# A fused retention and feed-forward kernel: constants and stores on GpSimd's DMA queue, one activation table, another order of weight pieces, chunk transposes and PSUM banks

## The chip, the cores and the metric

The kernel runs on one core of one Trainium2 chip. The metric is the device time of one execution in microseconds (us). The profile's span is about 1.8 us shorter than the time of the same execution, so I compare spans with spans and times with times.

Names: PE is TensorE's matmuls, PEld its weight loads, DVE is VectorE, ACT is ScalarE, POOL is GpSimd, SP is the engine that issues most DMAs. "ACTq" or "SPq" is such an engine's instruction queue. "[1.87 <-DVE W L372]" behind a line of the timeline means that the engine stood idle for 1.87 us until VectorE's instruction at line 372, which writes W, was done.

## The reference

Attention with a decaying state over four batches, eight heads and 768 steps, followed by a feed-forward layer with a sigmoid gate:

```python
gamma = 1.0 - 2.0 ** (-5.0 - np.arange(H))          # one decay per head
for t in range(S):
    state = gamma * state + outer(k[t], v[t])        # per batch and head, 64 x 64
    y[t]  = q[t] @ state / sqrt(D)
x = y.transpose(0, 2, 1, 3).reshape(B * S, H * D)    # 3072 x 512
h = x @ w_in                                         # 512 x 2048
out = (h / (1 + exp(-1.702 * h))) @ w_out            # 2048 x 512
```

(I have shortened it; q, k and v are float32 and the weights come as 64-bit floats, which the kernel narrows itself.)

## The kernel before

Time is cut into 24 chunks of 128 steps and these into six blocks of four chunks. For each chunk, TensorE transposes q and k (`turn`, line 225), makes scores (`pa`, line 257), VectorE multiplies them with a decay mask (line 263), TensorE makes the output and the state's update (lines 284 and 292, `finish`), and VectorE scales the output into `X` (line 296). The feed-forward layer of block 0 runs in units of 16 matmuls (`up0`, line 329); block 1 follows in `up1` (line 342). The later blocks and the product with `w_out` for all blocks (`pd`, line 432) take up most of the span.

The front, roughly the first 43 us: there the weights are fetched in pieces and each piece is narrowed from 64 to 32 bits by one ScalarE and six VectorE instructions:

```python
def narrow():                                       # lines 188 to 198, shortened
    act.activation(m, hi, AF.Abs, scale=2.0 ** 16)                      # L188
    dve.tensor_scalar(m, m, MOST, LEAST, op0=min, op1=max)              # L189
    dve.tensor_scalar(mu, mu, 3, None, op0=shift_left)                  # L191
    dve.scalar_tensor_tensor(hi, hi, SIGN, mu, op0=and, op1=or)         # L192
    dve.tensor_scalar(mu, hi, 0xFF800000, None, op0=and)                # L193
    dve.scalar_tensor_tensor(lo, lo, 2.0 ** -52, m, op0=mult, op1=mult) # L194
    dve.tensor_add(w, hi, lo)                                           # L198
    fetch()                                         # the next piece's DMA
```

The first two calls take half pieces (128 x 512), the later ones 128 x 1024. The loop that interleaves them with the first four chunks, before the change:

```python
load(0)
act.dma_start(cold, ...)                            # column decays
act.dma_start(rowd[...], ...)                       # row decays, two DMAs
act.dma_start(whole[...], ...)                      # four small DMAs
fetch(); load(1); fetch()
make_identity(nc, ident)
# ... mask from cold, 7 idle transposes
turn(0, ...)
for j in range(CB):                                 # CB = 4
    attend(j)
    narrow()
    turn(j + 1)
    # ...
    attend(None, j)                                 # finish(j); the last one with chunk 4's scores
    if j == 0: narrow()
    else:      up0(0, j - 1, "x")
for n, unit in enumerate(...):
    up0(*unit, "xy"[n % 2])                         # PSUM tag of each half unit
```

A PSUM tag ("x" or "y") has two buffers. The transposes of q and k use tag "y".

## Time and profile before

| | before |
|---|---|
| time, median | 711.3 us |
| span of the profiled run | 711.2 us |
| TensorE busy | 685.9 us, 96% |
| VectorE busy from 24 to 40 us | 14.66 of 16 us |

The profiled execution took 712.99 us, 1.7 more than the median. TensorE is the bound nearly everywhere, so the time is TensorE's busy time plus its holes. The prediction below shows the lines on which that rests. Two lines of VectorE's timeline before belong beside them: the X of chunk 0 and the mask product of chunk 3, which releases chunk 4's scores on TensorE (the third line).

```profile
17.29 0.69 DVE L296 TENSOR_TENSOR X<-py,rowd 128x512 f32<-128x512 f32 x1 [0.92 <-PE py L292]
...
43.19 1.27 DVE L263 TENSOR_TENSOR G<-pa,mask 128x512 f32<-128x512 f32 x2
...
44.61 1.10 PE L257 MATMUL pa<-G 64*64 64x128 f32 x32 [1.68 <-DVE G L263]
```

Chunk 4's scores on TensorE start at 44.61. I use that place as the end of the front, since TensorE is nearly always busy after it.

### The profile page before, as it was taken

The page shows a single profiled execution, that of the slowest core. Times are in us where ns is not written, and L with a number is a line of the kernel's source. Part 1 is how long each engine was busy: PE and PEld are TensorE (multiplying, and loading weights), DVE is VectorE, ACT ScalarE, POOL GpSimd, SP SyncE. Part 2 cuts the span into 40 slices and gives each one's busy share as a digit, 9 for nine tenths or more (in the row PEclk, how much of TensorE's full clock was granted, in tenths as well). Part 3 has the DMA queues.
Part 4 walks back from the last instruction along what each step waited for, and adds up shares of the span by engine and source line. Part 5 has one row for each costly group of instructions (what it writes and reads, how often), then busy time and mean ns, then how long its engine had stood idle before and what let it go on. Part 6 is the DMA issues. An engine that isn't in the chain of part 4 may idle for free.

```text
span 711.2 us, 11031 instructions
## 1 busy us (share of the span) xinstructions
PE 685.9 (96%) x4493; PEld 572.1 (80%) x4493; DVE 361.3 (51%) x520; ACT 126.5 (18%) x197; POOL 111.1 (16%) x99
## 2 busy tenths in 40 slices
PE   6689999999989999999999999999999999999997
PEld 5577776446878888888888888888888888888886
DVE  2997879995621652344463345264345272344241
ACT  2312222321000000332000233000233000233000
POOL 2221000000266221100132200032200042000030
PEclk9999999999999999999999999999999999999999
DMA  9996442521211224300333300323310220100001
GB/s 200 246 228 173 134 133 75 185 35 32 43 35 45 53 47 88 68 1 6 72 59 84 77 3 2 62 46 72 76 30 1 32 58 2 44 1 1 15 1 44
DMA packets 143602, 46.36 MB, mean 65 GB/s; under 512 B 130752, under 2 KB 137408, under 8 KB 143552
## 3 DMA queue, kind: packets, MB, share of 16 engines
q1 hardware_dynamic: 134704, 38.84, 23.9%
q10 hardware_dynamic: 8848, 6.83, 3.1%
q8 instruction: 35, 0.57, 0.3%
q14 instruction: 15, 0.12, 0.1%
HBM read 39.33 MB, written 6.29 MB: 64 GB/s over the span
## 4 chain that ended last, share of the span: by engine, by line
PE 81%; DVE 9%; SPq 5%; DMA 2%; issue 2%; ACT 1%; ACTq 0%; DVEq 0%
PE pd L432 34%; PE px L381 15%; PE py L381 11%; PE ph L342 8%; PE ph L329 5%; SPq L132 5%; PE py L284 3%; PE pa L257 3%; PE py L292 1%; PE py L282 1%; DVE G L371 1%; DVE W L198 1%; DVE G L263 1%; DMA W<-in_moe_w_in_dram 1%; DMA kn_in<-in_k_dram 1%
## 5 line engine op out<-in xcount | busy, mean ns | idle before, releaser
L432 PE MATMUL pd<-W,G 128*128 128x256 f32 x1120 | 247.4, 381 | 0.4 <-DVE G L372 0.3
L432 PEld LDWEIGHTS pd<-W,G 128*128 128x128 f32 x1120 | 211.3, 190 | 30.6 <-DVE G L372 1.2
L381 PE MATMUL px<-X,W 128*128 128x256 f32 x512 | 119.1, 379 | 1.2 <-ACT p L388 1.2
L381 PEld LDWEIGHTS px<-X,W 128*128 128x128 f32 x512 | 97.1, 190 | 14.9 <-POOL X L356 1.6
L381 PE MATMUL py<-X,W 128*128 128x256 f32 x384 | 90.7, 379 | 0.0
L381 PEld LDWEIGHTS py<-X,W 128*128 128x128 f32 x384 | 73.0, 190 | 9.9
L329 PE MATMUL ph<-X,W 128*128 128x256 f32 x256 | 57.9, 383 | 4.8 <-ACT G L226 4.1
L263 DVE TENSOR_TENSOR at<-pa,mask 128x512 f32<-128x512 f32 x32 | 21.7, 686 | 79.6 <-PE py L284 70.8
L329 PEld LDWEIGHTS ph<-X,W 128*128 128x128 f32 x256 | 47.8, 190 | 12.3 <-ACT G L226 4.8
L342 PE MATMUL ph<-W,W 128*128 128x512 f32 x128 | 55.1, 592 | 0.0
L244 POOL TENSOR_TENSOR kd<-kn_in,cold 128x512 f32<-128x512 f32 x13 | 13.6, 1044 | 237.5 <-PE py L292 182.4
L342 PEld LDWEIGHTS ph<-W,W 128*128 128x128 f32 x128 | 24.3, 190 | 30.2 <-issue 29.2
L373 POOL TENSOR_TENSOR G<-G 128x512 f32<-128x512 f32 x20 | 29.5, 1484 | 118.2 <-DVE G L372 115.4
L310 DVE TENSOR_TENSOR G<-G,sg 128x512 f32<-128x512 f32 x48 | 33.1, 689 | 14.0 <-ACT sg L308 14.0
L308 ACT ACTIVATE sg<-G 128x512 f32<-128x512 f32 x48 | 30.3, 631 | 49.4 <-DVE G L391 28.8
L308 ACT ACTIVATE sg<-ph 128x512 f32<-128x512 f32 x32 | 19.1, 598 | 104.2 <-PE ph L329 54.5
L432 PE MATMUL pd<-W,W 128*128 128x256 f32 x160 | 35.6, 380 | 1.9 <-DVE W L372 1.9
L432 PEld LDWEIGHTS pd<-W,W 128*128 128x128 f32 x160 | 30.2, 190 | 7.0 <-DVE W L372 2.3
L391 DVE TENSOR_TENSOR G<-py,p 128x512 f32<-128x512 f32 x16 | 11.1, 692 | 39.1 <-PE py L381 35.3
L419 ACT ACTIVATE u<-pd 128x512 f32<-128x512 f32 x6 | 3.6, 597 | 149.8 <-PE pd L432 149.8
L423 DVE TENSOR_TENSOR o<-pd,vv 128x512 f32<-128x512 f32 x12 | 7.7, 687 | 35.6 <-ACT vv L419 35.6
L405 DVE TENSOR_TENSOR G<-py,vv 128x512 f32<-128x512 f32 x16 | 11.1, 692 | 25.7 <-ACT vv L402 25.7
(97 smaller groups left out, 646.0 us busy)
## 6 DMA issues: line engine op xcount, KB each, us to landing
v_in<-in_v_dram SPq DMA_DIRECT2D x24, 256.0 KB, 4.2
W<-in_moe_w_in_dram SPq DMA_DIRECT2D x12, 512.0 KB, 5.2
out_dram<-o ACTq DMA_DIRECT2D x24, 256.0 KB, 2.4
W<-in_moe_w_out_dram SPq DMA_DIRECT2D x10, 512.0 KB, 4.2
q_sq<-in_q_dram SPq DMA_DIRECT2D x256, 16.0 KB, 1.8
k_sq<-in_k_dram SPq DMA_DIRECT2D x256, 16.0 KB, 1.8
kn_in<-in_k_dram SPq DMA_DIRECT2D x13, 256.0 KB, 3.9
G<-in_moe_w_out_dram SPq DMA_DIRECT2D x6, 512.0 KB, 4.1
```

Of the source, the lines that this page charges most:

```text
L132: tc.keep_in_program_order(sp.dma_start(t[r0:r0 + C4, hp], src[b, hp + HP * (r0 // D), rows, d0:d0 + C4].rearrange("(s p) d -> p s d", p=C4)))
L244: pool.tensor_mul(KD[j].rearrange("p (r s) d -> p r s d", r=2), x, cold[:, H:2 * H].rearrange("p (r s) -> p r s", r=2)[:, :, :, None].to_b ...
L257: pe.matmul(p[t, i, hp, :], kt[r, hp, t], qt[r, hp, :], start=True, stop=True)
L263: dve.tensor_mul(AT[j][:, i], p[:, i], mask[:, i])
L284: pe.matmul(out, vn[:, HP * r + s, :], a[:, r, s, :], start=(not c and s < 2), stop=(s >= 2), skip_group_check=True)
L308: act.activation(s, h, AF.Sigmoid, scale=1.702)
L310: dve.tensor_mul(g, h[:, i], s[:, i])
L329: pe.matmul(h[:, ab], w, X[:, 2 * half + c // 2, c % 2, :], start=(ab == 0 and c == 0), stop=(c == 3), skip_group_check=True)
L342: pe.matmul(h, w, X1[:, c // 2:4:2, c % 2, :], start=(c == 0), stop=(c == 3))
L373: pool.tensor_sub(a[1], a[1], a[0])
L381: pe.matmul(acc[:, u, :], W1[:, 2 * d + u, sa, c, :], X[:, sb, c, :], start=(start and u == 0 and c == 0), stop=(stop and c == 1), skip_gr ...
L432: pe.matmul(p0[:, n, :], g1(m, p, sa)[:, n * P:(n + 1) * P], W2[:, sb, p, :], start=(new and p == 0 and n == 0), stop=(last and p == NP - ...
```

## The change

The intent: make the first scores start sooner (ScalarE no longer issues the constants' DMAs and loads its table at once), save the second activation table load (the trace of the kernel before has two, of 1.28 us each), keep a half piece of weights from standing in front of chunk 1's mask, keep block 0's units out of the PSUM buffers that the transposes use, give VectorE cover for its sums, and take the stores off ScalarE. The core of the diff:

```diff
-            act.dma_start(rows[th, e], o)
+            (pool if m < NB - 1 else act).dma_start(rows[th, e], o)
 ...
     load(0)
-    act.dma_start(cold, col_decay[:, 0:2 * H])
-    act.dma_start(rowd[0:D], ...)
-    act.dma_start(rowd[D:P], ...)
-    (four act.dma_start of whole)
+    make_identity(nc, ident)
+    pool.dma_start(cold, col_decay[:, 0:2 * H])
+    (two pool.dma_start of rowd)
+    first = const.tile([P, 1], F32, name="first")
+    dve.memset(first, 0.0)
+    act.activation(first, first, AF.Sigmoid)
     fetch()
     load(1)
     fetch()
-    make_identity(nc, ident)
 ...
     turn(0, lambda: keep_warm(3))
+    (four pool.dma_start of whole, kept in program order)
 ...
         attend(j)
         narrow()
+        if j == 1:
+            narrow()
         turn(j + 1)
 ...
-        if j == 0:
-            narrow()
-        else:
+        if j:
             up0(0, j - 1, "x")
 ...
-        up0(*unit, "xy"[n % 2])
+        up0(*unit, "xxyx"[n % 4])
 ...
-            between = [lambda: turn(2 * CB), lambda: attend(2 * CB), lambda: turn(2 * CB + 1)]
+            between = [lambda: turn(2 * CB), lambda: attend(2 * CB), lambda: None, lambda: None, lambda: turn(2 * CB + 1)]
```

More of the change, by code (lines that the diff above doesn't have):

```diff
@@ L464 @@
     load(0)
-    act.dma_start(cold, col_decay[:, 0:2 * H])
-    act.dma_start(rowd[0:D], bass.AP(tensor=row_decay.tensor, offset=row_decay.offset, ap=[[0, D], [2 * P, HP], [1, P]]))
-    act.dma_start(rowd[D:P], bass.AP(tensor=row_decay.tensor, offset=row_decay.offset + P, ap=[[0, D], [2 * P, HP], [1, P]]))
-    W = 2 * H + HP
-    for r in range(2):
-        for i in range(2):
-            act.dma_start(whole[r * D:(r + 1) * D, :, i],
-                          bass.AP(tensor=col_decay.tensor, offset=col_decay.offset + i * D * W + 2 * H + 2 * r,
-                                  ap=[[W, D], [1, 2]]))
+    make_identity(nc, ident)
+    pool.dma_start(cold, col_decay[:, 0:2 * H])
+    for i in range(2):
+        pool.dma_start(rowd[i * D:(i + 1) * D], bass.AP(tensor=row_decay.tensor, offset=row_decay.offset + i * P,
+                                                        ap=[[0, D], [2 * P, HP], [1, P]]))
+    first = const.tile([P, 1], F32, name="first")
+    dve.memset(first, 0.0)
+    act.activation(first, first, AF.Sigmoid)
     fetch()
@@ L501 @@
     turn(0, lambda: keep_warm(3))
+    W = 2 * H + HP
+    for r in range(2):
+        for i in range(2):
+            tc.keep_in_program_order(pool.dma_start(
+                whole[r * D:(r + 1) * D, :, i],
+                bass.AP(tensor=col_decay.tensor, offset=col_decay.offset + i * D * W + 2 * H + 2 * r,
+                        ap=[[W, D], [1, 2]])))
     for _ in range(2):
```

## The prediction

> **What bounds the kernel now.** I read the page of the profile first (busy shares, slices), then busy time by stretch, then the timeline wherever TensorE (PE) has a hole, then the chain that ended last.
>
> ```profile
> span 711.2 us, 11031 instructions
> PE 685.9 (96%) x4493; PEld 572.1 (80%) x4493; DVE 361.3 (51%) x520; ACT 126.5 (18%) x197; POOL 111.1 (16%) x99
> PE   6689999999989999999999999999999999999997
> PE 81%; DVE 9%; SPq 5%; DMA 2%; issue 2%; ACT 1%; ACTq 0%; DVEq 0%
> ```
>
> PE is busy for 685.9 of 711.2 us, so all that reordering can win is its 25.3 us of idle time, plus what matmuls lose when they run slowly after a hole. The slices put the holes into the first tenth of the span and the last slice. The stretches (window length, PE busy) say how many:
>
> ```profile
> 0.00:12.00 12.00, 5.56 (x33) 4.79 (x37) 1.18 (x8) 2.93 (x4) 2.81 (x8) 1.00 0.81 172
> 12.00:24.00 12.00, 8.75 (x130) 7.13 (x124) 9.42 (x17) 2.97 (x5) 3.19 (x3) 0.96 1.08 287
> 24.00:40.00 16.00, 13.61 (x147) 11.53 (x144) 14.66 (x20) 5.21 (x6) 3.84 (x3) 0.93 0.87 236
> 684.00:712.00 28.00, 22.86 (x105) 19.68 (x104) 3.05 (x5) 1.19 (x2) 1.27 (x1) 1.00 0.09 29
> ```
>
> Idle PE: 6.4 us in 0 to 12, 3.3 in 12 to 24, 2.4 in 24 to 40, 3.0 in 40 to 60, then 1.4 each in 60 to 80 and 80 to 115, 1.9 in 170 to 199, 1.2 in 245 to 287. The last window runs 0.8 us past the span, so its hole is 4.3 us (last sums and stores), and the change leaves that alone. From 287 to 684 there is 0.1 us: nothing to win there.
>
> The timeline and the waits name each hole:
>
> ```profile
> 8.99 1.28 ACT L226 ACT_TABLE_LOAD   x1 [8.99 <-DMA whole<-in_col_decay_dram]
> 11.42 1.99 PE L257 MATMUL pa<-G 64*64 64x128 f32 x32 [3.26 <-ACT G L226]
> 22.43 0.43 PE L284 MATMUL py<-G,v_in 128*64 128x128 f32 x2 [2.48 <-DVE G L263]
> 56.99 7.17 PE L329 MATMUL ph<-X,W 128*128 128x256 f32 x32 [1.32 <-ACT G L226]
> 198.69 1.99 PE L432 MATMUL pd<-W,W 128*128 128x256 f32 x8 [1.87 <-DVE W L372]
> 286.76 1.59 PEld L381 LDWEIGHTS px<-X,W 128*128 128x128 f32 x8 [1.59 <-POOL X L356]
> 286.79 1.97 PE L381 MATMUL px<-X,W 128*128 128x256 f32 x8 [1.22 <-ACT p L388]
> SPq L118 <- DMA cold<-in_col_decay_dram: 3.1, 1, 3.1
> ```
>
> Line one: ACT issues the constants' DMAs until 8.96, so its table load and first copies out of PSUM come late and chunk 0's scores start at 11.42. The holes like that at 56.99 are three (at 57.0, 76.5 and 95.6; 1.32 + 1.37 + 1.37 = 4.1 us): a half unit takes the PSUM tag "y" that the two transposed tiles have just used.
>
> [...] both show 1283 ns (one for copies, one at L308 for the sigmoid). [...] in 193.5 to 198.6 the DVE sums take 1.64 to 1.75 us beside GpSimd's, against 0.69 alone. [...]
>
> **The change, part by part.**
>
> *Constants to GpSimd, early table load.* [...] Today chunk 1's q load waits for "cold" (3.1 us, quoted) and starts at 7.60. After, [...] it follows W at once. Step by step: ACT issues k until 1.85, loads the table until about 3.2 and is free. PE transposes q0 at 4.94 (its load is unchanged) and k0 until 7.5; two copies of 0.6 us each; chunk 0's scores start near 8.2 instead of 11.42: 3.2 us. The mask: "cold" no longer queues behind k0, lands near 4.5 to 5; 8 DVE copies 1.2 us; GpSimd's select 1.1 us[...]: ready near 7, in time for scores ending near 9.6. The first 12 us then lean on the DMA. Up to k1 it must carry six 256 KB blocks (q, k, v, the row decays, q1, k1) and W's 512 KB: 2.1 MB from about 2.2 us on, at some 240 GB/s (the 2 us windows from 2 to 8 us show 217 to 270), puts k1 near 11 instead of 13.0. So chunk 0's second matmuls start near 11.4 (before: 15.23) and X near 13.1 (17.29).
>
> *Second half piece behind chunk 1's mask.* Before, chunk 1's mask (L263) waits on DVE among seven operations of the second half piece, and PE waits 2.48 + 0.77 us, then runs slowly (16 matmuls of L292 in 1.17 us against 0.68). In the new order only one 0.7 us add lies between the two mask products. I follow DVE, which is the pacemaker of 13 to 45 us (14.66 of 16 us busy): mask 1 done near 17.1 (before 23.6), then the half piece with X and state between: 5 us, to 22.1. The first unit's last matmuls now wait for it (two of the eight calls may go ahead), so part is handed back. It ends near 25.4 (30.97); the next piece and mask 2 are done near 30.6 (35.6). So 5.0 us arrive at 35; DVE's order from there is the same, so they also arrive at PE's 44.6. The DMA (share 0.87 to 1.08) may not keep up; v2's landing near 30.3 today is the tight one. I take 4.6 us.
>
> *PSUM order.* "xxyx" gives the unit after each transpose an "x" bank. Removed: 4.1 us. Does a new wait arise? That unit needs the bank of the unit two before it. From 64.16 (end of the earlier unit) DVE releases that bank at 74.3, 10.2 us later; PE gets there after 3.0 (attention) + 3.6 + 3.6 + 0.9 = 11.1 us. Margin 0.9 us. One later case gives 9.7 against 10.8. DVE would be some 90% busy, hence 3.9 us.
>
> *Transposes of chunk 9 moved by six units.* In 186.5 to 198.7 they cost DVE 1.3 us ahead of the sums that PE waits 1.87 for. The GpSimd subtraction that ran beside the transposes will now slow sums instead (0.9 us each). I take 1.2 us.
>
> *Outputs through GpSimd.* 20 of 24 stores leave ACT, whose block at 275.7 to 285.6 held the copy "p" that PE waited for at 286.79. But look at the line above it: the weight load waited for GpSimd's X until 286.76, so nearly the same hole stays. Gain 0.4 us. [...]
>
> Sum: 4.6 + 3.9 + 1.2 + 0.4 = 10.1 us; 711.2 - 10.1 = 701.1.
>
> **The rivals.** *A: the DMA is the real bound of the first 45 us.* For: shares near 1 and landings of 5 to 7 us. Against: no PE hole in 12 to 45 us names a DMA, and between 9 and 11 us the DMA has free slices because the loads were issued late. If so the front gives 2 us, not 4.6: 703.7. *B: the holes come back elsewhere.* The margins of 0.9 us at the "x" banks are eaten because DVE slows, or GpSimd, waiting in order for a store's tile, delays X, kd or state. For: GpSimd already gates PE at 286.76. Against: GpSimd is busy 16% of the span and waits up to 58.6 us at a time for PE. Giving back half of the middle and 2 us in the steady part: 705. *C: everything fits.* All holes named above close: the front 6.0, 4.1, 1.9, 1.2: 13.2 us, 698.0. *D: [...]* If a GpSimd DMA takes several us, "cold" and the mask come after 10 and scores wait: front gain 1 us, 705.
>
> **Range and chances.** Centre 701.0. A to D span 698 to 705, so 698.2 to 704.8 for eight in ten. Faster by over 2% needs under 697.0, that is 14.2 us, more than all holes named (13.2) unless slow matmuls near 25 us count too: 6%. Slower by over 2% would need over 14 us of new stalls: 1%. Within 2%: 93%.
>
> **What would show it.** Chunk 0's scores (L257) begin near 8.2; only one table load; no ACT wait on "whole"; chunk 1's second matmuls near 17 without a 2.5 us hole; the first L342 matmul near 106 instead of 114.6; no L329 wait on L226; a hole of at most 1 us near 188 and still about 1 us near 276 on GpSimd's X; a tail of the same 4.3 us. It would be wrong if PE waits for loads or for the mask in the first 20 us, if L329 waits on L310, or if holes appear between 287 and 684.

## The result

| | before | changed | ratio, 95% interval |
|---|---|---|---|
| first look, 4 runs each | 711.31 (709.88 to 712.86) | 703.87 (703.46 to 704.61) | 0.9896 [0.9874, 0.9919] |
| once more (e5 below), 5 and 11 runs | 712.72 (708.92 to 713.58) | 703.13 (701.63 to 704.33) | 0.9872 [0.9852, 0.9893] |

Ratios are computed as the mean time of one kernel's fast runs over that of the other's of the same rounds, so they are not quite the ratio of the medians beside them. The change saves 1.0 to 1.3%, 7.4 to 9.6 us by the medians. By the 2% limit that is "within 2%", as predicted; the predicted 701.0 is 2 to 3 us too low and the range 698.2 to 704.8 holds the result.

The page of the changed kernel: the header, the busy line, TensorE's slices and granted clock, and the chain that ended last.

```profile
span 701.9 us, 11046 instructions
PE 686.3 (98%) x4493; PEld 572.5 (82%) x4493; DVE 361.5 (52%) x521; ACT 125.8 (18%) x197; POOL 129.7 (18%) x126
PE   6799999999999999999999999999999999999997
PEclk9899999999999999999999999999999999999999
PE 93%; DVE 5%; DMA 1%; ACT 0%; SPq 0%; issue 0%; ACTq 0%
```

TensorE has the same work (686.3 us against 685.9) in a shorter span; the notches of the third and twelfth slices are gone. SP's queue and the issue of DMAs have left the chain. GpSimd has 19 us more to do, most of it the 20 stores at 744 ns each.

The same stretches as in the prediction (window, then PE, PEld, DVE, ACT and POOL busy, granted clock, DMA share, GB/s):

```profile
0.00:12.00 12.00, 6.96 (x59) 6.12 (x60) 3.98 (x14) 3.43 (x6) 7.52 (x16) 0.93 0.89 202
12.00:24.00 12.00, 9.05 (x130) 7.02 (x129) 8.57 (x15) 4.13 (x6) 2.85 (x4) 0.93 1.00 298
24.00:40.00 16.00, 14.21 (x124) 11.13 (x126) 15.34 (x17) 2.87 (x6) 4.98 (x4) 0.79 0.89 250
```

TensorE is busier in them than before by 1.4, 0.3 and 0.6 us. The granted clock has fallen, from 0.93 to 0.79 in the third, so part of that busy time is the same matmuls run slowly. And VectorE is busy 15.34 of 16 us there. Both are taken up by the experiments.

The places that answer to those of the prediction, in the timeline:

```profile
1.92 1.28 ACT L473 ACT_TABLE_LOAD   x1 [1.92 <-issue]
7.70 1.10 PE L257 MATMUL pa<-G 64*64 64x128 f32 x32 [0.36 <-ACT G L226]
10.79 1.09 PE L225 MATMUL pt<-ident,q_in 128*128 128x128 f32 x4 [1.99 <-DMA q_in<-in_q_dram]
14.77 0.69 DVE L296 TENSOR_TENSOR X<-py,rowd 128x512 f32<-128x512 f32 x1 [3.02 <-PE py L292]
42.74 1.10 PE L257 MATMUL pa<-G 64*64 64x128 f32 x32 [0.80 <-ACT G L226]
53.63 7.07 PE L329 MATMUL ph<-X,W 128*128 128x256 f32 x32
190.74 1.99 PE L432 MATMUL pd<-W,W 128*128 128x256 f32 x8 [0.28 <-DVE W L372]
277.46 1.89 PE L381 MATMUL px<-X,W 128*128 128x256 f32 x8
```

There is one table load, at 1.92. Chunk 0's scores start at 7.70 instead of 11.42. TensorE then waits 1.99 us for chunk 1's q. The units of block 0 run without the three waits on transposed tiles, `pd`'s wait for VectorE's sums is 0.28 instead of 1.87 us, and the wait in the first matmuls of block 2 (1.22 us) is gone.

To see where the 9.3 us of span came from, I cut the spans at places that every run has: the start of chunk 4's scores, the first `pd` matmuls that read `g` ("the first sums" from here on; 189.76 before, 183.04 changed), the first `px` matmuls of block 2, and the end.

| stretch | before | changed | gain | predicted |
|---|---|---|---|---|
| start to chunk 4's scores | 44.61 | 42.74 | 1.87 | 4.6 |
| to the first sums | 145.15 | 140.30 | 4.85 | 3.9 |
| to block 2's first px | 92.20 | 90.97 | 1.23 | 1.2 |
| to the end | 429.24 | 427.89 | 1.35 | 0.4 |
| sum (span) | 711.2 | 701.9 | 9.3 | 10.1 |

Three of the four terms came in at least as large as predicted. The front brought less than half. The two traces differ by 9.3 us and the medians of the first look by only 7.4, since the profiled execution of the kernel before was a slow one; the front's 1.87 us may therefore be too high, and there is no second trace of the kernel before. So the question for the experiments: why is a 3.7 us earlier start worth 1.9 us at chunk 4?

### The profile page after: what moved, and what is told of

It is laid out like the page before. It is cut to its first block, busy times and chain, and to the rows that moved or that the text cites. A ratio compares the mean times of both kernels' runs of the same rounds, so it can differ in the third digit from the quotient of the medians.

```text
span 701.9 us, 11046 instructions
## 1 busy us (share of the span) xinstructions
PE 686.3 (98%) x4493; PEld 572.5 (82%) x4493; DVE 361.5 (52%) x521; ACT 125.8 (18%) x197; POOL 129.7 (18%) x126
## 4 chain that ended last, share of the span: by engine, by line
PE 93%; DVE 5%; DMA 1%; ACT 0%; SPq 0%; issue 0%; ACTq 0%
PE pd L432 39%; PE px L381 16%; PE py L381 12%; PE ph L329 8%; PE ph L342 8%; PE py L284 4%; PE pa L257 3%; PE py L292 1%; PE py L282 1%; DMA q_in<-in_q_dram 1%; DVE W L371 1%; DVE G L371 1%; PE pt L225 1%; DVE G L372 1%; DVE W L372 1%; DVE W L198 0%
## 5 line engine op out<-in xcount | busy, mean ns | idle before, releaser
L329 PE MATMUL ph<-X,W 128*128 128x256 f32 x256 | 60.9, 397 | 1.6 <-DVE W L198 0.9
L329 PEld LDWEIGHTS ph<-X,W 128*128 128x128 f32 x256 | 49.9, 199 | 9.7 <-DVE W L198 1.3
L342 PE MATMUL ph<-W,W 128*128 128x512 f32 x128 | 55.1, 592 | 0.0
L342 PEld LDWEIGHTS ph<-W,W 128*128 128x128 f32 x128 | 24.3, 190 | 30.2 <-issue 29.2
L310 DVE TENSOR_TENSOR G<-G,sg 128x512 f32<-128x512 f32 x48 | 33.0, 688 | 13.7 <-ACT sg L308 13.7
L424 POOL DMA_DIRECT2D out_dram<-o x20 | 14.9, 744 | 128.5 <-DVE o L423 128.5
```

The costliest lines, as they stand in the source:

```text
L310: dve.tensor_mul(g, h[:, i], s[:, i])
L329: pe.matmul(h[:, ab], w, X[:, 2 * half + c // 2, c % 2, :], start=(ab == 0 and c == 0), stop=(c == 3), skip_group_check=True)
L342: pe.matmul(h, w, X1[:, c // 2:4:2, c % 2, :], start=(c == 0), stop=(c == 3))
L424: (pool if m < NB - 1 else act).dma_start(rows[th, e], o)
```

## The experiments

All twelve gave correct results. They were in four groups, each with its own runs of the kernel before. The same cuts for all of them, so that each can be looked up (the last column is the ratio to the kernel before, with its interval):

| run | chunk 4's scores | to sums | to px | to end | median us | ratio |
|---|---|---|---|---|---|---|
| before | 44.61 | 145.15 | 92.20 | 429.24 | 711.3 | |
| changed | 42.74 | 140.30 | 90.97 | 427.89 | 703.87 | 0.9896 [0.9874, 0.9919] |
| e1 old PSUM order | 44.73 | 145.45 | 90.97 | 427.85 | 709.14 | 0.9963 [0.9936, 0.9990] |
| e2 old constants | 42.71 | 140.30 | 90.96 | 428.03 | 705.00 | 0.9912 [0.9881, 0.9943] |
| e3 old pieces | 43.18 | 140.30 | 90.97 | 427.85 | 703.50 | 0.9876 [0.9846, 0.9906] |
| e4 old stores | 42.96 | 140.29 | 90.96 | 428.69 | 704.43 | 0.9897 [0.9872, 0.9922] |
| e5 changed again | 41.89 | 140.30 | 90.96 | 428.15 | 703.13 | 0.9872 [0.9852, 0.9893] |
| e6 fillers | 42.06 | 140.30 | 90.96 | 427.98 | 702.62 | 0.9860 [0.9838, 0.9882] |
| e7 q and k first | 42.89 | 140.30 | 90.96 | 427.95 | 701.37 | 0.9856 [0.9834, 0.9878] |
| e8 old transposes | 43.10 | 140.30 | 92.21 | 428.09 | 705.51 | 0.9902 [0.9883, 0.9921] |
| e9 more VectorE work | 44.35 | 141.87 | 90.97 | 427.81 | 705.75 | 0.9916 [0.9894, 0.9939] |
| e10 two adds on GpSimd | 40.20 | 140.34 | 90.97 | 428.19 | 701.99 | 0.9863 [0.9839, 0.9888] |
| e11 fillers, q and k first | 39.66 | 140.30 | 90.98 | 427.86 | 700.62 | 0.9847 [0.9825, 0.9870] |
| e12 all three | 38.58 | 140.30 | 90.97 | 427.85 | 699.87 | 0.9823 [0.9794, 0.9851] |

The columns to the sums and to px repeat to a few hundredths and the last one to 0.4 us, unless the edit touches them. The first one doesn't: the changed kernel's own front, which e1, e4, e5 and e8 leave alone, took 41.89 to 44.73 us in five traces (42.74, 44.73, 42.96, 41.89, 43.10; mean 43.1). A single trace of the front therefore shows only differences of some 2 us.

The record also has the span of every execution, not only of the profiled one. If the three later stretches last as long in all executions of a kernel as in its trace, a span less their sum is an estimate of where chunk 4's scores came:

| kernel | executions | estimated start of chunk 4's scores, mean (range) | in the trace |
|---|---|---|---|
| before | 43 | 43.7 (39.9 to 46.7) | 44.61 |
| front as changed (changed, e1, e4, e5, e8) | 27 | 42.6 (40.4 to 44.7) | 41.89 to 44.73 |
| e2 old constants | 6 | 43.9 (42.2 to 46.1) | 42.71 |
| e3 old pieces | 6 | 42.0 (39.4 to 44.0) | 43.18 |
| e6 fillers | 5 | 41.3 (40.4 to 42.1) | 42.06 |
| e7 q and k first | 5 | 40.8 (39.8 to 42.9) | 42.89 |
| e9 more VectorE work | 6 | 43.0 (40.8 to 44.4) | 44.35 |
| e10 two adds on GpSimd | 5 | 40.3 (38.8 to 41.0) | 40.20 |
| e11 fillers, q and k first | 4 | 39.6 (39.4 to 39.8) | 39.66 |
| e12 all three | 5 | 39.0 (38.2 to 39.6) | 38.58 |

The estimate is rough (the last stretch alone differs by 0.4 us between traces, and the groups ran on different chips, with 43.1 to 44.5 for the kernel before), but it shows where a trace was of an untypical execution. By it the front as changed gained about 1.1 us, not 1.9. Across chips, ratios are a safer comparison than medians: e1 to e4 ran on one chip, e5 to e8 on a second, e9 to e12 on a third.

### e1, e2, e3, e4: each part taken back

e1 puts the PSUM tags back:

```diff
-        up0(*unit, "xxyx"[n % 4])
+        up0(*unit, "xy"[n % 2])
```

> The changed kernel with block 0's old PSUM tags (x, y in turn), nothing else. Theory 1 (the traces: the three holes of 1.3 to 1.4 us and the late starts beside them cost 4.8 us between chunk 4's scores and the first L342 matmul): the three L329 waits on L226 come back, time 703.9 + 4.8 = 708.7 us, ratio to before 0.996. Rival (VectorE is nearly full in this stretch, so the holes only moved there): it costs 2 us or less, 705.5 us.

It took 709.14 us. The waits view of TensorE (us in total, times, longest) has the three waits again, and the stretch to the sums is 145.45 instead of 140.30:

```profile
PE ph L329 <- ACT G L226: 4.3, 3, 1.7
```

The tags are worth 5.15 us by the trace, 0.9 more than the waits that the line counts. This is the largest part of the change.

e2 gives the constants' DMAs back to ScalarE, takes out the early activation, and so has the late first table load (at 7.89) and the second one (at 24.77):

```diff
-    pool.dma_start(cold, ...)       # and rowd, whole; and the activation of "first"
+    act.dma_start(cold, ...)        # and rowd, whole
```

> The changed kernel with the constants on ScalarE's queue and the table load behind them, as before; half pieces, PSUM tags, stores and transposes stay changed. Theory 1 (the start of chunk 0 sets VectorE's chain of the first 45 us): chunk 0's scores start at 11.4 instead of 7.7, about 2.5 us of it survive to chunk 4's scores, time 706.4 us. Rival (chunk 1's loads and the clock set the chain, the early start is lost in any case): 704.4 us or less.

It took 705.00 us. The timeline of TensorE, chunk 0's and chunk 4's scores:

```profile
10.32 1.99 PE L257 MATMUL pa<-G 64*64 64x128 f32 x32 [2.02 <-ACT G L226]
...
42.71 1.10 PE L257 MATMUL pa<-G 64*64 64x128 f32 x32 [1.68 <-DVE G L263]
```

Chunk 0's scores are 2.6 us later than in the changed kernel, chunk 4's come at the same time. The early start of the constants, the most elaborate part of my prediction, is not to be seen at the end of the front in this trace, which is of one of the faster executions of e2. The estimates from all executions leave it 1.3 us (43.9 against 42.6), the medians 1.1 us (against the first look) or 1.9 us (against e5, on another chip), with intervals that overlap. The second table load, which is in this run too, costs nothing that shows.

e3 puts the second half piece back to its old place:

```diff
-        if j == 1:
-            narrow()
 ...
-        if j:
+        if j == 0:
+            narrow()
+        else:
             up0(0, j - 1, "x")
```

> The changed kernel with the second half piece ahead of chunk 1's mask again. Prediction's view: a hole of about 2.5 us comes back in front of chunk 1's second matmuls and most of it reaches the end, 706.3 us. Rival (VectorE is the pacemaker and does the same work in another order): the hole comes back but the time rises by 0.5 us or less, 704.4 us.

It took 703.50 us, the same as the changed kernel. The long hole before chunk 1's second matmuls is back, and yet chunk 4's scores come at 43.18:

```profile
21.07 0.43 PE L284 MATMUL py<-G,v_in 128*64 128x128 f32 x2 [1.88 <-DVE G L263]
...
43.18 1.10 PE L257 MATMUL pa<-G 64*64 64x128 f32 x32 [1.68 <-DVE G L263]
```

So this part gains nothing that can be measured. A hole of TensorE was closed in one place, and as much waiting opened in others (the changed kernel waits 0.69, 0.86, 0.49 and 1.30 us in the same stretch).

e4 has the stores on ScalarE's queue again:

```diff
-            (pool if m < NB - 1 else act).dma_start(rows[th, e], o)
+            act.dma_start(rows[th, e], o)
```

> The changed kernel with all stores on ScalarE's queue. Theory 1 (ScalarE's block behind the third store is what made the hole before the third product of block 2): the hole of 1.2 us comes back, 705.1 us. Rival (the hole hangs on when kn lands and GpSimd finishes X, as the prediction said): no change beyond 0.4 us, 703.9 us, and the hole is there or not by the landing of kn.

It took 704.43 us, which can't be told from the changed kernel by its time. The trace can tell: the stretch to the end is 0.80 us longer, and it is one hole,

```profile
278.72 1.97 PE L381 MATMUL px<-X,W 128*128 128x256 f32 x8 [0.89 <-ACT p L388]
```

The stores are worth 0.8 us, twice what I had predicted (0.5 to 0.9 us against the other runs of that stretch, 427.81 to 428.19).

### e5: the changed kernel again, and e8: the old place of chunk 9's transposes

> The changed kernel once more, as the yardstick of this group. The first look gave 703.9 us (four runs), a ratio of 0.990. Both theories expect 703 to 705 and a ratio of 0.988 to 0.992. What it is for: how far the front moves by itself from run to run. If chunk 4's scores, at 42.74 in the first trace, start over 1 us earlier or later here, then differences of that size between the traces of other runs show nothing about their edits.

703.13 us. The front was 0.85 us shorter than in the first trace, with one stretch of half clock in place of three (below).

e8:

```diff
-            between = [..., lambda: attend(2 * CB), lambda: None, lambda: None, lambda: turn(2 * CB + 1)]
+            between = [..., lambda: attend(2 * CB), lambda: turn(2 * CB + 1)]
```

> The changed kernel with the transposes of chunk 9 back at their old place before the first sums of block 0. My theory (they left no matmuls to lie beside the eight additions of VectorE, and this cost 1.6 us): the wait of L432 for W (0.28 us at 190.74) is 1.7 to 2 us again and the time is 1.2 to 1.9 us more than the changed kernel of this group. Rival (the transposes only filled a hole that another wait would have made, since TensorE must run them anyway): the wait returns but something later shrinks, and the time is within 0.5 us.

705.51 us, 2.4 more than e5. The wait is back (same place and columns as above):

```profile
192.35 1.99 PE L432 MATMUL pd<-W,W 128*128 128x256 f32 x8 [1.88 <-DVE W L372]
```

The stretch around it is 92.21 us, that of the kernel before (92.20), against 90.97. The transposes are worth 1.24 us: the 1.6 us of the wait less 0.36 us that the sums next to it lose. The other 1.2 us of e8's trace lie in the front, where it was not edited (43.10 against 41.89).

### e6, e7: half clock and late data as suspects

In the changed kernel's front I had two suspects. TensorE's granted clock fell to 0.5 three times, at 10.3 to 13.7, 23.9 to 27.3 and 34.2 to 37.6, against once before (22.9 to 26.3). And chunk 1's q, loaded behind a weight piece on SP's queue, landed late.

e6 puts idle transposes into the thin stretches:

```diff
+        if j == 0: keep_warm(12)              # after attend(0)
+                   keep_warm(5), keep_warm(9) # among the second matmuls of chunks 1 and 2
+                   keep_warm(6), keep_warm(6) # before and within the first unit
+        if j == 2: keep_warm(4)               # before chunk 2's end
```

> The changed kernel with idle transposes put into the thin stretches of the first 36 us (12 after chunk 0's scores, 5 and 9 among the second matmuls of chunks 1 and 2, 6 before and 6 within the first unit, 4 before chunk 2's end). Theory 1 (TensorE falls to half clock three times, 10.4 to 13.8, 23.9 to 27.3 and 34.4 to 37.8, since thin work precedes them, and this eats much of the early start): at most one such stretch is left, the first unit's 12 matmuls take under 3.9 us instead of 4.54, chunk 4's scores start 1 to 1.9 us earlier than in the changed kernel of this group, and the ratio falls by 0.0015 to 0.003. Theory 2 (VectorE sets the pace of the front, and half clock falls in time that TensorE would have waited anyway): the half-clock stretches go, but chunk 4's scores move by less than 0.7 us and the ratio by less than 0.001. If half clock stays in spite of the fillers, neither is told apart.

702.62 us; 0.5 below e5, whose interval it shares. The fillers held the clock up everywhere but from 19.5 to 22.9 (the expectation of e11 below puts this stretch wrongly at 20.8 to 24), behind a wait of 1.50 us for chunk 2's k. That one stretch lay on the path: chunk 1's X came 2.25 us late for VectorE. Chunk 4's scores at 42.06 are within what the unedited front shows. By what I had written down, half clock stayed and neither theory is told apart.

e7 changes the order of the loads:

```diff
+    load(1, "qk")
     fetch()
-    load(1)
+    load(1, "v")
```

> The changed kernel with chunk 1's q and k loaded ahead of the first weight piece instead of after it, and its v after that piece. Theory 1 (the early scores of chunk 0 are lost to the landing of chunk 1's q and k, on which the transposes waited 1.99 us at 10.79, because Sync's queue was never part of the change): the transposes begin at 9.3 to 9.8, X of chunk 0 on TensorE (14.77) comes 1 to 1.7 us earlier, and chunk 4's scores come 0.8 to 1.7 us earlier, unless the first unit now waits longer for its weights (it waited 0.86 us for W), which would take that back. Theory 2 (the pace of VectorE from chunk 1's mask to chunk 2's end decides): X comes earlier, chunk 4's scores do not, by more than 0.5 us.

701.37 us, 1.8 below e5 by the median, though the intervals overlap. The transposes begin at 8.87 without a wait and X of chunk 0 comes at 13.02, as theory 1 had it. Chunk 4's scores stayed at 42.89, as theory 2 had it. VectorE waited four times between, 3.75 us in all: 1.40 us for chunk 1's output, 1.66 us for the sigmoid of the first unit, which ran at half clock (0.50 from 25 to 27 us), 0.49 and 0.20 us. In this run TensorE itself waited 1.71 us for the weights that now land later. But the profiled execution was the slowest of the five (703.98 us; the others took 700.81 to 702.02). By the estimate from all five, chunk 4's scores came 1.0 us earlier than in e5 (40.8 against 41.8), which is within theory 1's 0.8 to 1.7. So e7 does not exclude theory 1.

### The count that fits all runs

Comparing these traces I noticed what the stretch from chunk 0's X to chunk 4's scores consists of. I took from VectorE's timeline its start (X), and the waits that it lists in that stretch:

| run | X of chunk 0 | X to chunk 4's scores | VectorE's listed waits | rest |
|---|---|---|---|---|
| before | 17.29 | 27.32 | 1.13 | 26.2 |
| changed | 14.77 | 27.97 | 1.37 | 26.6 |
| e1 | 15.90 | 28.83 | 2.01 | 26.8 |
| e2 | 15.95 | 26.76 | 0.85 | 25.9 |
| e3 | 15.92 | 27.26 | 1.08 | 26.2 |
| e4 | 15.74 | 27.22 | 0.49 | 26.7 |
| e5 | 13.84 | 28.05 | 1.25 | 26.8 |
| e6 | 13.74 | 28.32 | 2.25 | 26.1 |
| e7 | 13.02 | 29.87 | 3.75 | 26.1 |
| e8 | 15.07 | 28.03 | 1.83 | 26.2 |

The rest is 25.9 to 26.8 us in all ten, whatever was edited. So the front is the time of X, plus some 26.4 us of VectorE's work, plus VectorE's waits. This is bookkeeping and proves no cause: VectorE runs the same instructions between the two places in all ten, and the rest also holds their slowing beside GpSimd (the changed kernel's L189 at 24.08 took 1.38 us instead of 0.69) and the 0.15 to 0.31 us from its last mask product to the scores. That VectorE's work sets the pace can be tested directly, by giving it more and less to do.

The waits are where TensorE's clock comes in. In all five traces of the front as changed the second unit ran partly at half clock (4.90 to 5.11 us against 3.72 before) and VectorE waited for its sigmoid in each (0.48 to 1.01 us). What released chunk 4's scores in the end was then not VectorE's mask, as before, but ScalarE's copy of chunk 4's transposed k (the lines at 44.61 and 42.74 above). So at the very end of the changed front the chain through the slow unit came last, 0.3 us behind VectorE.

The lists of all executions point the same way: e3's took 698.5 and 699.2 us of span at a mean granted clock of 0.999 and 0.998, and 701.5 to 703.1 us at 0.992 to 0.995. In the first look's four runs no such order shows, and the lists don't tell cause from effect.

### e9, e10: VectorE's work changed

e9 repeats the clamp of line 189, which changes no result, four times in all:

```diff
+        if i in (2, 4):
+            for _ in range(2):
+                dve.tensor_scalar(m, m, F64_MOST * 2.0 ** 16, F64_LEAST * 2.0 ** 16, op0=ALU.min, op1=ALU.max)
         dve.tensor_scalar(mu, mu, 3, None, op0=ALU.logical_shift_left)
```

> The changed kernel with four more VectorE instructions between 24 and 36 us: the clamp of line 189, which gives the same result when it is done again, twice more for each of the first two wide weight pieces; 4 x 0.69 = 2.8 us of work for VectorE and nothing for any other engine. Theory 1 (from chunk 0's X, at 14.77 or 13.84 in the two traces of the changed kernel, to chunk 4's scores VectorE sets the pace; the distance was 27.97 and 28.05 us there, 27.32 before, 27.26 with the old order of pieces): chunk 4's scores come 2.2 to 2.8 us later and the time is 2 to 2.8 us more than the changed kernel's 703.1 to 703.9. Theory 2 (TensorE at half clock or the landing of data sets it): VectorE has slack, and chunk 4's scores and the time move by less than 1 us.

705.75 us, 2.6 more than e5 and 1.9 more than the first look. X came at 14.07, chunk 4's scores at 44.35 (lines are three further down in this kernel):

```profile
44.35 1.99 PE L260 MATMUL pa<-G 64*64 64x128 f32 x32 [2.38 <-DVE G L266]
```

The distance is 30.28 us, 2.25 more than the 28.0 of the two traces of the changed kernel. Instructions for no engine but VectorE moved TensorE's path in this trace. By the count above, some 1.0 us of it are longer VectorE waits (2.32 us in all) and some 1.2 us are work, since the second wide addition (1.21 us) slipped behind the last mask product in the order that the scheduler chose. The profiled execution was the slowest of six; by the ratios e9 took 1.4 to 3.1 us more than the changed kernel (0.9916 against 0.9896 and 0.9872). The stretch to the sums grew as well, by 1.57 us: one more half-clock stretch begins there at 44.

e10 gives the last addition of the first two wide pieces to GpSimd:

```diff
-        dve.tensor_add(w, hi, lo)
+        (pool if i in (2, 4) else dve).tensor_add(w, hi, lo)
```

> The changed kernel with the last addition of the first two wide weight pieces (1.22 and 1.52 us of VectorE, line 198) on GpSimd. Theory 1 of the run before: VectorE has 2.7 us less to do; GpSimd's two additions should take some 2.1 us each (its 128x512 multiplication takes 1.04) and slow VectorE's work beside them, as happened beside lines 244 and 301, by an estimated 1 to 1.5 us together; chunk 4's scores come 0.8 to 2 us earlier than 41.9 to 42.7, the time falls by as much. Theory 2: they stay within 0.5 us. A third outcome: contention takes all of it, and they come later.

701.99 us, 1.1 below e5 and 1.9 below the first look. GpSimd's timeline and TensorE's:

```profile
30.44 1.89 POOL L198 TENSOR_TENSOR W<-W 128x1024 f32<-128x1024 f32 x1 [5.08 <-DVE W L194]
```

```profile
40.20 1.10 PE L257 MATMUL pa<-G 64*64 64x128 f32 x32 [1.32 <-DVE G L263]
```

X came late in this run (15.28), and still chunk 4's scores came at 40.20: 24.92 us, 3.1 less than the changed kernel, with no VectorE wait listed. GpSimd's two additions take 1.89 us each; VectorE's work beside them is slower (the L189 at 31.48 takes 1.41 us instead of 0.69), yet the sum is well below what VectorE was spared. Of the 3.1 us, 1.7 to 1.9 are a smaller rest, out of 2.7 us spared, and 1.3 are waits that the changed kernel had and this trace has not (its clock fell only once, from 12.4 to 15.7, and both units ran at full clock). Both tests went the way of theory 1: in the front VectorE's work counts nearly in full. How much of the difference is a luckier clock is not separated.

### e11, e12: what the theory makes possible

e11 has the edits of e6 and e7 together.

> The changed kernel with both earlier edits: idle transposes in the thin stretches, and chunk 1's q and k loaded first. Alone, the first gave chunk 4's scores at 42.06 (its fillers kept the clock at 1.0 from 24 us on, but a half-clock stretch at 20.8 to 24 remained), the second 42.89 (X of chunk 0 at 13.02, then 1.71 us lost to the wait for the weights and 1.66 us of VectorE waiting for the first unit at half clock). Theory 1 (VectorE sets the pace, and its 27.3 us start at chunk 0's X as long as nothing holds it up): X at 13.0, chunk 4's scores at 40.3 to 41.3, time 0.5 to 1.5 us below the changed kernel's. Theory 2 (the landing of weights is what holds after 20 us, whatever the order): chunk 4's scores at 42 or later.

700.62 us, its runs within 700.38 to 700.73. The three front stretches:

```profile
0.00:12.00 12.00, 9.21 (x84) 8.10 (x86) 3.45 (x12) 4.32 (x7) 8.12 (x16) 1.00 0.93 242
12.00:24.00 12.00, 9.62 (x139) 7.92 (x137) 11.66 (x21) 3.20 (x5) 3.85 (x4) 1.00 1.07 311
24.00:40.00 16.00, 14.19 (x179) 11.61 (x181) 15.76 (x19) 5.51 (x8) 1.74 (x3) 1.00 0.89 231
```

The granted clock is 1.00 throughout and VectorE is busy for 11.66 of 12 and 15.76 of 16 us: no wait is left in it. Chunk 4's scores come at 39.66, below the expected 40.3 to 41.3, and the time is 2.5 to 3.2 us below the changed kernel's instead of 0.5 to 1.5; X comes at 14.35 with 1.1 us of weight work already done before it. In the traces it looks as if each edit alone had lost its gain to a wait that the other one removes: the fillers lacked the data in time (e6), the early data met a first unit at half clock (e7). The times don't bear this out. Against e5 the medians fell by 0.5 us (e6), 1.8 us (e7) and 2.5 us (both), the ratios by 0.0012, 0.0016 and 0.0025: within the noise the two gains add. That e7 and e11 differ in nothing but the fillers (estimated fronts of 40.8 and 39.6) is the best sign here that half clock costs something at the end.

e12 adds e10's edit.

> The changed kernel with all three edits that moved the front: idle transposes, chunk 1's q and k first, and the two wide additions on GpSimd. The second and third together with the first gave chunk 4's scores at 39.66 (first and second) and 40.20 (third alone), against 41.89 to 42.74 in the changed kernel. Theory 1 (VectorE sets the pace; what is taken from it comes off, less the contention): another 1 to 1.6 us below the kernel with two edits, chunk 4's scores at 38.0 to 38.7 and 699.0 to 699.8 us. Rival (the two remedies use the same slack: with TensorE at full clock the fixed chain of chunk by chunk matmuls or the landing of weights takes over): 39.3 to 39.8 and 700.3 to 700.9 us.

699.87 us (699.13 to 700.60), chunk 4's scores at 38.58. By the trace another 1.08 us, at the edge of the expected 1 to 1.6, by the median 0.75. In this trace the last release before chunk 4's scores is ScalarE's copy again (0.80 us), and VectorE waits 0.95 us for a sigmoid, so the rival's limit is near. The ratio to the kernel before is 0.9823, with an interval on both sides of the 2% limit (the verdict is "unclear"), and by the medians it is 3.3 to 4.0 us faster than the changed kernel (e5, on another chip, and the first look; the runs don't overlap). This version beats both kernels.

## Why the prediction was right or wrong

**The bound and the class: right.** TensorE's work stayed at 686 us, all gains came from its holes, and they add to about 1%. That the sum of 10.1 us came so close to the 9.3 us of the traces is in part luck: the front fell short by 2.7 us, and the other three parts exceeded their forecasts by 1.9 us together, for reasons that I had not foreseen.

**PSUM order: right in mechanism, 3.9 predicted, 4.85 measured before against after, 5.15 in e1.** I had subtracted for margins of 0.9 us at the "x" buffers; no wait on them appeared (rival B). The 0.9 us beyond the listed waits lie between the transposes and the units after them; I have not taken them apart.

**Transposes of chunk 9: right, 1.2 predicted, 1.23 and 1.24 measured.** The wait shrank by 1.6 us and the sums beside GpSimd's work took 0.36 us of that back, the kind of loss that I had foreseen.

**Stores: wrong in the reason, 0.4 predicted, 0.8 measured in e4.** I expected nearly the same hole to stay, since GpSimd's X came as late as ScalarE's copy. With the stores off ScalarE both came sooner: in the six traces that I looked at (changed, e2, e5, e6, e8, e10) no wait of the matmuls above 0.3 us was left there. X came sooner because its chain on GpSimd starts with line 244, which waits for the landing of `kn`: that came 0.14 us before the first `px` matmuls in the kernel before, 1.46 us in the changed kernel and 0.81 us in e4. Why `kn` landed sooner I have not isolated; that the stores' place decides both is shown by e4, where both waits return. The other 0.55 us of that stretch's 1.35 I can't assign.

**Front: the step that failed, 4.6 predicted, 1.9 measured in the first trace, 2.7 in the second, 1.5 against the mean of five traces, about 1.1 by the estimates from all executions.** My sentence was "So 5.0 us arrive at 35; DVE's order from there is the same, so they also arrive at PE's 44.6." That is, X at 13.1 and chunk 4's scores near 40.0. Two terms of it were mis-sized. The sizes below compare with the one trace of the kernel before.

*X of chunk 0.* Predicted 13.1, measured 13.84 to 15.90 in the five traces, on average 15.1. That is 2.0 of the 3.1 us missing. The transposes of q waited for their data to 10.8 or later, and chunk 1's k was there at 11.6 (e5) instead of "near 11"; at full clock X then came 0.7 us late. Then the clock: where it was full at that time (e5, e9), X came at 13.84 and 14.07; where it fell to half between 10 and 17 (changed, e1, e3, e4, e8, e10), X came at 14.77 to 15.92. The prediction saw slow matmuls near 25 us and took them for a consequence of the hole there; no step and no rival expected half clock elsewhere.

*From X to chunk 4.* I counted on 26.9 us, 0.4 less than before, because the new order of half pieces closes TensorE's hole before chunk 1's second matmuls. It was 28.0 on average over the five traces, 0.7 more than before: the other 1.1 us. The prediction itself named VectorE as "the pacemaker of 13 to 45 us". Taking that at its word would have given the answer: another order of the same VectorE work can shorten its path by VectorE's waits at most, and before there was one of 1.13 us. With the old order of pieces (e3) the distance was 27.26 us, no longer than with the new one. Of the 0.7 us that were lost, 0.3 are longer waits of VectorE (1.39 us on average over the five traces, against 1.13), since the slow first and second units now made it wait for sigmoids, and 0.4 are a longer rest. Of these, 0.15 are the longer way from the last mask product to the scores, which ScalarE's copy now ends. One thing that the rest contains is instructions slowed beside GpSimd; the first trace shows both:

```profile
24.08 1.38 DVE L189 TENSOR_SCALAR W<-W 128x1024 f32<-128x1024 f32 x1 [0.51 <-ACT W L188]
25.49 0.98 DVE L191 TENSOR_SCALAR W<-W 128x1024 uint32<-128x1024 uint32 x1
...
28.84 0.69 DVE L310 TENSOR_TENSOR W<-ph,sg 128x512 f32<-128x512 f32 x1 [0.37 <-ACT sg L308]
```

The first two take 0.69 us each when GpSimd is idle; GpSimd ran its lines 244 and 301 from 23.86 to 25.92. The kernel before has such instructions too (its L189 at 27.11 takes 1.08 us), so I can't assign the remaining 0.3 us to them.

**What I said would show it.** Chunk 0's scores at 7.70 (8.2 predicted), one table load, no hole of 2.5 us before chunk 1's second matmuls, no L329 waiting for L226, a hole of 0.28 us at the sums, a tail of 4.3 us again: as predicted. Not as predicted: the first L342 came at 107.88 instead of 106, which is the front's loss less the PSUM order's surplus, and no wait of 1 us was left in block 2. One sign of being wrong that I had named also came true: TensorE waited for loads in the first 20 us, 2.5 us for q (1.99 at 10.79) and 0.3 for k. Two small readings in the prediction are off: ScalarE's block of stores ends at 285.9, not 285.6, and the slow and the fast group of line 292 have 13 matmuls each, not 16.

**Rival A** (the DMA is the bound of the first 45 us, front gain 2 us, 703.7) hit the time best, but not as I had it. The data's landing decides when X comes; after X no listed wait of VectorE in the two traces of the changed kernel goes back to the DMA but the 0.28 us of e5, and e9 and e10 move the end of the front with the DMA left as it is. In e6, though, the late k of chunk 2 was on the path. **D** fell: GpSimd's DMAs cost it 0.60 to 0.75 us each, and `cold` had landed by 5.0.

What stays open: when the clock falls in a given run (one to three times in the same front), how much each fall costs at the end (so the split of the front's loss between VectorE's work and half clock is argued, not shown), and how much of the constants' earlier start survives (nothing at chunk 4 in e2's single trace, 1.1 to 1.9 us by its median). The early table load alone was not tried; only e2 has it, with the constants.

## What to carry to other kernels

Where TensorE has holes, ask which engine does not, in that stretch alone: here TensorE was 98% busy over the span, but the first 43 us ran nearly at VectorE's pace, and an earlier start of its work, less of it, or fewer waits in it moved the end. Reordering the pacemaker's own work (e3) closed a hole and opened others. A profile shows one execution: where a stretch differs by 2 us from one execution to the next, check with all spans whether the profiled one is typical before reading a cause from it (e7's was the slowest of five). Two remedies whose gain alone could not be told from the noise (e6, e7) gave 2.5 us together against e5, about the sum of their medians' gains, so try the pair before giving up either.

## What the traces show of half clock and of GpSimd's DMAs

- In the first 40 us, each fall of the granted clock to 0.5 lasted 3.4 us or 6.8 (the longer ones in e4, e8 and e9: 10.3 to 17.2, 31.2 to 38.0 and 30.6 to 37.5, by the mean clock of windows of 1 us). What sets a fall off is not shown. In the changed kernel's first trace TensorE's longest hole after its first matmul is 1.99 us, and it fell three times (at 10.3, 23.9 and 34.2), while a hole of 3.26 us in the kernel before (ahead of 11.42) was followed by no fall. The 3.4 us ahead of two of the three falls had TensorE busy about half the time, 1.78 of 3.42 and 1.79 of 3.41 us in the lines below (window, PE busy, and so on as above; the second runs 0.2 us into the fall). That gives no threshold either: in e2 a stretch with 1.62 of 3.41 us busy (31.00 to 34.41) was followed by a clock of 1.00 up to 40 us.

```profile
20.55:23.97 3.42, 1.78 (x15) 1.15 (x10) 2.86 (x6) 1.09 (x1) 0.10 (x1) 0.99 0.95 267
31.00:34.41 3.41, 1.79 (x30) 1.55 (x31) 3.34 (x6) 0.00 (x0) 0.00 (x0) 0.96 0.60 149
```

- The count of falls differs from trace to trace of the same front: one (e5) to three (the first trace, e1), with fronts from 41.89 to 44.73 us. The whole change is 1% here, so a study of single traces needs several of them.
- A DMA issued from GpSimd cost it, in the changed kernel's trace, 0.60 us for one of 0.5 KB, 0.70 for one of 8 KB, 0.63 for one of 128 KB and 0.744 for a store of 256 KB. From these stores' issue to landing it was 2.7 us (median); ScalarE's stores in the kernel before took 2.4.
- In the kernel before, chunk 1's q load on SP's queue waited 3.1 us for the landing of `cold`; in the changed kernel that wait is gone. Why it waited is not shown by the traces.
